# Attention outputs made transposed on column halves of TensorE, normalised before the product

## The chip, the cores and the metric

The kernel runs on one core of a Trainium2 chip. A core has five engines with an instruction queue each: TensorE (in the profile PE for its products and PEld for its weight loads), VectorE (DVE), ScalarE (ACT), GpSimd (POOL) and SyncE (SP), which here only issues transfers. Sixteen DMA engines move data. SBUF is the working memory on 128 partitions; PSUM, which takes TensorE's results, has eight banks of 2 KB per partition. Each engine executes its queue in order and waits at semaphores for the others. The metric is the device time of one execution in microseconds (us); 1 ns is a thousandth of that.

A TensorE product takes a stationary operand, loaded as weights, of up to 128 rows and 128 columns, and streams a moving operand through it: each moving column gives one result column, and the weights' columns become the partitions of the result.

## The reference

Two parts follow one another. First attention with 8 batch elements, 8 heads, 512 local and 32 global tokens, 64 numbers per head. A local token sees the 32 global tokens and the local ones at a distance of at most 32; a global token sees all 544. Then a layer of 8 experts over the 4352 resulting rows, weighted by a matrix P that eight rounds of row and column normalisation balance.

```python
s_g = scale * q_g @ k_all.T;  out_g = sm(s_g) @ v_all
s_ll = where(|i - j| <= 32, scale * q_l @ k_l.T, -1e9)
s_l = concat([scale * q_l @ k_g.T, s_ll]);  out_l = sm(s_l) @ concat([v_g, v_l])
# sm: exp(s - max) / (sum(exp(s - max)) + 1e-9)
x = concat([out_g, out_l])          # 4352 rows of 8 * 64
P = exp(x @ w_gate - max); 8 times: P /= rowsum; P /= colsum; P *= 4352 / 8
out = sum over e of P[:, e] * (relu(x @ w1[e]) @ w2[e])
```

## The kernel before

**Units.** One unit n is a batch element b and a pair of heads hp, 32 in all (four to a batch element). Its 512 queries are cut into eight blocks of 64, and one block of both heads makes 128 rows: partitions 0 to 63 are the first head's queries, 64 to 127 the second's. For that the queries stand in `qbd` block-diagonally. A block sees a window of 128 local keys and the 32 global ones, so a row of its scores has 160 numbers.

**Stages of a unit**, each a function:

- st_A transposes queries and keys into `qbd` and `kTe` (TensorE, L272, then VectorE and ScalarE copies).
- st_B makes the scores of three, three and two blocks (parts 0 to 2) on TensorE; VectorE adds the mask and takes the row's maximum in one instruction (L304, with a small read of the accumulator); ScalarE takes the exponential into `Pu` (L307). The exponentials aren't divided by their sum here. st_B0 is a form of st_B for the first four units, with the mask added by a product (L326) and one maximum per part (L331).
- st_D1 copies the 32 global columns of each row into `Pl` (POOL, L341), transposes the 128 local ones on TensorE (L344) into `ptw`, and VectorE copies the result to `pw` (L346). st_D2 transposes `Pl` (L352), and ScalarE copies it to `pg` (L354).
- st_E makes the outputs in two halves, for the even and the odd blocks (par 0 and 1): per block a product with `pw` as weights and the values as moving operand (L375) and one with `pg` and the global values (L377), accumulated into `po`. The weights' columns are the rows of both heads, and the moving operand has the values of both heads, 65 columns each: the 65th is a column of ones, so that it yields the sum of the exponentials. VectorE takes the reciprocals of the sums (L380) and multiplies the two quarters of the result that belong together into `xn` (L383).
- st_X transposes `xn` (L361), and ScalarE copies it into `xT` (L362), the transposed input of the expert layer.

Values stand in `va` (even blocks' windows), `vb` (odd blocks') and `vgz`, in which the global values stand once in each quarter of the partitions with zeros around; each has 65 columns per head.

**Global queries**, 16 groups of a batch element and four heads: st_G0 lays out queries (POOL), st_G1 makes the scores of 128 rows and 544 columns, their maximum (L408) and exponential `Pg` (L411), st_G2 transposes `Pg` (L419) into `pgs`, st_G3 makes the outputs of all four heads with five products of 260 columns (L431, L432) and scales the four matching pieces into `xgn`, by turns on ScalarE and VectorE (L441, L444); st_G4 transposes `xgn` twice in the kernel (L449) and copies it into `xT`.

**Order.** The whole order is written by hand; every engine takes its instructions in the order in which the program makes them. Units 0 to 3 are made in a first loop (L551), in which inputs land and are cast on POOL (L129, L145), and values are selected by products (L152). There the global keys of the first batch element are transposed on 32 rows of TensorE (L547), and later, at step 4, the global queries and keys of all elements on 64 rows (transpose_g: loads L192, casts on POOL L197, transposes L201). From step 4 on (loop at L601) step s does st_X of unit s - 2, st_D1, st_D2 and st_E of unit s - 1, st_B of unit s and st_A of unit s + 1. Between them stand the products of experts 0 and 1: f1 gives four products for one tile of hidden rows (p_l1, L470, relu on ScalarE or VectorE as its argument says), f2 eight products for one tile of outputs (p_l2, L484, copied by ScalarE at L487). st_G1 comes at the end of steps 4, 5, 6, 7 and every odd step from 9 to 31 (`gat`), st_G2 and st_G3 in the step after. In such a step st_D1 stands first, then two f1, st_B part 0, st_D2, st_G2. POOL also issues the value loads of the next batch element and casts its queries and keys at the end of steps.

**PSUM.** Two banks each for `mm` (p_l1, p_l2, gate logits), `sc` (scores, global outputs), and `tr` (all transposes; the tiles `pt` and `ptw`); `po` is one tile of two banks, which st_G1's scores use too. A tile waits until the readers of the earlier one in its place have ended.

After the attention follow the balancing of P, with rest work of experts 0 and 1 between its rounds, and the experts 2 to 7 (products L772 and L808 with sums and differences of operands), from about 413 us to the end.

## Time and profile before

| What | us |
|---|---|
| median of 3 runs | 1086.7 (1085.76 to 1090.41) |
| the profiled execution | 1088.94, span 1087.2 |
| TensorE busy (PE) | 1050.2, 97% of the span |
| VectorE, ScalarE, POOL busy | 697.7 (64%), 540.2 (50%), 126.6 (12%) |
| TensorE's mean granted clock | 0.991 |

All times in the profile count from the span's start. A group of instructions is named by its line, engine and operation, then what is written and read by the program's names (`po<-vb,pw`), the operands' shapes, a count, the busy time and the mean length in ns of one, and the idle time of the engine before them with what ended it. In the timeline, a line is a start, the time from the first start to the last end, and a group of up to that many like instructions in a row. TensorE pipelines its products: one of 128 moving columns is listed with 219 ns, and the next starts 56 ns later, so what a product costs the queue is the distance of starts, not its length.

### The profile page before, as it was taken

To read this page: it belongs to the slowest core of one execution; us is meant where nothing else is said; L and a number is where in the kernel's file an instruction comes from. 1 tells how busy PE (TensorE), PEld (TensorE's weight loads), DVE (VectorE), ACT (ScalarE), POOL (GpSimd) and SP (SyncE) were. 2 spreads that over 40 slices of the span, in tenths; PEclk is the share of its full clock that TensorE was granted. 3 is DMA by queue.
4 is the path that set the end of the run, shared out by engine and by line. 5 is a ranking of instruction groups with operands and counts; after the bars stand their busy time and mean duration, and the time that the engine had idled before them with its cause. 6 is when DMAs were issued, how large, how long until landed. Compare 5 with 4: busy or idle time off the path is not lost.

```text
span 1087.2 us, 19737 instructions
## 1 busy us (share of the span) xinstructions
PE 1050.2 (97%) x7988; PEld 685.3 (63%) x7988; DVE 697.7 (64%) x1504; ACT 540.2 (50%) x1091; POOL 126.6 (12%) x232
## 2 busy tenths in 40 slices
PE   7689999999999999999999999999999999999987
PEld 4555665666665455666666666666666666666676
DVE  6667676767676666768457466576575474485474
ACT  5658777777766445334334334343343343343332
POOL 7251332231401500000000000000000000000000
PEclk8989999999999999999999999999999999999999
DMA  9956676785753977423423424524424334234242
GB/s 257 195 99 168 101 170 184 114 181 145 136 103 66 215 172 289 184 97 137 174 98 136 175 97 141 185 87 175 179 99 173 137 136 175 97 136 144 104 169 79
DMA packets 102963, 160.55 MB, mean 148 GB/s; under 512 B 40909, under 2 KB 75865, under 8 KB 91865
## 3 DMA queue, kind: packets, MB, share of 16 engines
q1 hardware_dynamic: 52376, 120.03, 32.4%
q0 software_dynamic: 46736, 20.20, 15.3%
q10 hardware_dynamic: 3760, 19.08, 4.5%
q8 instruction: 62, 1.02, 0.4%
q14 instruction: 29, 0.23, 0.1%
HBM read 149.24 MB, written 33.40 MB: 168 GB/s over the span
## 4 chain that ended last, share of the span: by engine, by line
PE 81%; DVE 9%; DMA 3%; ACT 2%; issue 2%; SPq 1%; POOL 0%; DVEq 0%; ACTq 0%; POOLq 0%
PE ph L772 32%; PE m L808 20%; PE pm L808 8%; PE ph L470 8%; PE py L484 7%; DVE xn L383 3%; DMA qgf<-in_q_g_dram 1%; DVE hT L475 1%; PE sc L297 1%; PE po L377 1%; DVE ms L304 1%; PE po L375 1%; DMA pb<-pd 1%; SPq L192 1%; ACT yst L487 1%
## 5 line engine op out<-in xcount | busy, mean ns | idle before, releaser
L774 ACT ACTIVATE h<-ph 128x512 f16<-128x512 f32 (+1 forms) x432 | 247.1, 573 | 397.7 <-PE ph L772 393.8
L772 PE MATMUL ph<-xs,w1s 128*128 128x512 f16 (+1 forms) x1728 | 405.3, 367 | 3.6 <-DMA w1s<-w1d 2.3
L772 PEld LDWEIGHTS <-w1s 128*128 128x128 f16 x1728 | 169.0, 98 | 128.3 <-issue 2.6
L814 DVE SCALAR_TENSOR_TENSOR o<-pm,o 128x512 f32<-128x512 f32 (+1 forms) x106 | 70.6, 667 | 241.3 <-PE pm L808 241.0
L808 PEld LDWEIGHTS <-h 128*128 128x128 f16 x1616 | 158.1, 98 | 48.4
L808 PE MATMUL m<-w2c,s 128*128 128x256 f16 x1212 | 158.3, 273 | 0.0
L808 PEld LDWEIGHTS <-s 128*128 128x128 f16 x1212 | 118.6, 98 | 43.8
L470 PE MATMUL ph<-xT,w1e 128*128 128x512 f16 (+1 forms) x576 | 135.2, 368 | 3.7 <-DVE lg L459 1.4
L484 PE MATMUL py<-w2e,hT 128*128 128x512 f16 x544 | 128.3, 379 | 0.1
L708 DVE TENSOR_TENSOR xs<-xT,pb 128x2048 f16<-128x2048 f16 (+2 forms) x57 | 117.2, 2060 | 11.1 <-DMA pb<-pd 11.1
L808 PE MATMUL m<-w2c,h 128*128 128x256 f16 x808 | 105.5, 273 | 0.0
L808 PE MATMUL pm<-w2c,h 128*128 128x256 f16 x808 | 96.9, 273 | 0.0
L708 DVE TENSOR_TENSOR s<-h 128x2048 f16<-128x2048 f16 (+1 forms) x106 | 92.3, 912 | 4.5 <-ACT h L774 4.5
L470 PEld LDWEIGHTS <-w1e 128*128 128x128 f16 x576 | 54.6, 99 | 51.5 <-issue 6.8
L484 PEld LDWEIGHTS <-hT 128*128 128x128 f16 x544 | 50.8, 97 | 51.0 <-issue 0.2
L307 ACT ACTIVATE Pu<-ms,mx 128x160 f16<-128x160 f32 x224 | 80.8, 422 | 3.2 <-DVE mx L304 1.7
L304 DVE CUSTOM_DVE_ANT_0 ms<-sc,mask 128x160 f32<-128x160 f32 x224 | 59.7, 321 | 34.6 <-PE sc L299 17.9
L708 DVE TENSOR_TENSOR h<-h 128x1024 f16<-128x1024 f16 (+1 forms) x106 | 65.6, 660 | 0.0
L383 DVE TENSOR_TENSOR xn<-po,rr 64x256 f16<-64x256 f32 x128 | 54.0, 422 | 3.1
L473 ACT ACTIVATE hT<-ph 128x512 f16<-128x512 f32 (+1 forms) x91 | 48.9, 564 | 13.8 <-PE ph L470 11.4
L814 DVE SCALAR_TENSOR_TENSOR o<-m,o 128x512 f32<-128x512 f32 (+1 forms) x90 | 52.2, 653 | 0.4
L487 ACT COPY yst<-py 128x512 f32<-128x512 f32 x68 | 39.5, 581 | 21.0 <-PE py L484 18.7
(156 smaller groups left out, 971.1 us busy)
## 6 DMA issues: line engine op xcount, KB each, us to landing
w1s<-w1d SPq DMA_DIRECT2D x54, 1024.0 KB
yd<-yst ACTq DMA_DIRECT2D x16, 1024.0 KB
pb<-pd SPq DMA_DIRECT2D x48, 256.0 KB
o<-yd SPq DMA_DIRECT2D x8, 1024.0 KB
y<-yd SPq DMA_DIRECT2D x8, 1024.0 KB
out_dram<-o SPq DMA_DIRECT2D x8, 1024.0 KB
f<-in_q_l_dram SPq DMA_DIRECT2D x15, 512.0 KB
f<-in_k_l_dram SPq DMA_DIRECT2D x15, 512.0 KB
```

Of the source, the lines that this page charges most:

```text
L304: nc.vector.tensor_tensor_reduce(out=ms[:, ii, :], in0=sc[:, SW * ii : SW * (ii + 1)], in1=mask[:, mi, :], scale=-scale, scalar=BIG, op0=A ...
L307: nc.scalar.activation(out=d["Pu"][:, i, :], in_=ms[:, ii, :], func=AF.Exp, scale=-1.0, bias=d["mx"][:, i : i + 1])
L383: nc.vector.tensor_tensor(out=d["xn"][HB * par : HB * (par + 1), :, Dh * a : Dh * (a + 1)], in0=po[r, :, VW * a : VW * a + Dh], in1=rr[r]. ...
L470: nc.tensor.matmul(ph[:, 0:n], wts[e][0][:, dk, P * fm : P * (fm + 1)], xT[:, dk, c0 : c0 + n], start=(dk == 0), stop=(dk == DP - 1))
L473: nc.scalar.activation(out=hT[:, fm, 0:n], in_=ph[:, 0:n], func=AF.Relu)
L484: nc.tensor.matmul(py, hT[:, fk, P * c : P * (c + 1)], wts[e][1][:, fk, :], start=(fk == 0), stop=(fk == FT - 1))
L487: nc.scalar.copy(out=ys[:, c, :], in_=py)
L708: nc.vector.tensor_tensor(out=out, in0=in0, in1=in1, op=op)
L772: nc.tensor.matmul(ph[:, 0:n], w1s[i][:, dk, P * fm : P * (fm + 1)], xss[i][:, dk, 0:n], start=(dk == 0), stop=(dk == DP - 1))
L774: nc.scalar.activation(out=hs[i][:, fm, 0:n], in_=ph[:, 0:n], func=AF.Relu)
L808: nc.tensor.matmul(pm[:, HD * t : HD * (t + 1)], lhs[0][:, k, lhs[1] + P * t : lhs[1] + P * (t + 1)], w[:, q - 1, k, :], start=(k == 0 and ...
L814: nc.vector.scalar_tensor_tensor(out=o, in0=pm[:, 0 : HD * nt].rearrange("p (t d) -> p t d", d=HD), scalar=sg / float(E), in1=o, op0=ALU.m ...
```

## The change

The probabilities are divided by their sums before they meet the values, and the outputs come out of TensorE transposed.

- The exponentials on ScalarE (st_B, st_B0, st_G1) also give the sum of the row (`accum_out`), into `sm` and into a column of `m2`.
- A new stage st_N takes the reciprocals (VectorE, three, three and two at a time) and multiplies the 128 local columns of each block in place (VectorE, one instruction per block); after the last part POOL makes `Pl`, which it copied in st_D1 before, as the product of the 32 global columns and the reciprocals. st_GN does the same for a group's `Pg`: reciprocal and one multiplication on VectorE.
- st_E has the values as weights and the probabilities as moving operand: per block and head one product with 64 columns of weights and 64 moving columns, and another with the global values. The first head's results go to partitions 0 to 63, the second's to 64 to 127, so each uses one half of TensorE's columns. Both halves of blocks go into one `po` of one bank, and ScalarE copies it straight into `xT`. Reciprocals, scalings, st_X and its step are gone.
- st_G3 makes per pair of heads five products with the two heads' values as 128 columns of weights and 64 moving columns; ScalarE and VectorE copy one part each into `xT`. st_G4 and `xgn` are gone.
- The columns of ones and their memsets are gone: `va`, `vb` and `vgz` have 64 columns per head.

```diff
-                nc.scalar.activation(out=d["Pu"][:, i, :], in_=ms[:, ii, :], func=AF.Exp, scale=-1.0,
-                                     bias=d["mx"][:, i : i + 1])
+                nc.scalar.activation(out=d["Pu"][:, i, :], in_=ms[:, ii, :], func=AF.Exp, scale=-1.0,
+                                     bias=d["mx"][:, i : i + 1], accum_out=d["sm"][:, i : i + 1])
+        def st_N(n, part):
+            d = st[n]
+            i0 = 3 * part
+            i1 = min(i0 + 3, NHB)
+            if part == 0:
+                d["rs"] = att_wk.tile([P, NHB], FP32, tag="rs", name="rs")
+            nc.vector.reciprocal(out=d["rs"][:, i0:i1], in_=d["sm"][:, i0:i1])
+            for i in range(i0, i1):
+                nc.vector.tensor_scalar(out=d["Pu"][:, i, 0:KW], in0=d["Pu"][:, i, 0:KW], scalar1=d["rs"][:, i : i + 1],
+                                        scalar2=None, op0=ALU.mult)
+            if part == 2:
+                d["Pl"] = att_wk.tile([P, NHB, Sg], FP16, tag="Pl", name="Pl")
+                nc.gpsimd.tensor_tensor(out=d["Pl"], in0=d["Pu"][:, :, KW:SW],
+                                        in1=d["rs"].unsqueeze(2).to_broadcast([P, NHB, Sg]), op=ALU.mult)
         def st_D1(n):
-            d["Pl"] = att_wk.tile([P, NHB, Sg], FP16, tag="Pl", name="Pl")
-            nc.gpsimd.tensor_copy(out=d["Pl"], in_=d["Pu"][:, :, KW:SW])
...
-        def st_X(n):
-            pt = ps_tr.tile([P, NJ, P], FP16, tag="tr")
-            for j in range(NJ):
-                nc.tensor.transpose(pt[:, j, :], xn[:, j, :], identity)
-            nc.scalar.copy(out=xT[:, hp, Sl * b : Sl * (b + 1)], in_=pt.rearrange("p j q -> p (j q)"))
         def st_E(n, par):
             if par == 0:
-                d["xn"] = att_wk.tile([P, NJ, P], FP16, tag="xn", name="xn")
-            po = ps_po.tile([P, NJ, 256], FP32, tag="po")
+                d["po"] = ps_po.tile([P, Sl], FP32, tag="po", name="po")
+            po = d["po"]
             for j in range(NJ):
                 i = 2 * j + par
-                nc.tensor.matmul(po[:, j, 0 : 2 * VW], d["pw"][:, i, :], vx[:, j, 2 * hp : 2 * hp + 2, :],
-                                 start=True, stop=False)
-                nc.tensor.matmul(po[:, j, 0 : 2 * VW], d["pg"][:, i // 4, :], vz[:, i % 4, 2 * hp : 2 * hp + 2, :],
-                                 start=False, stop=True)
-            rr = att_wk.tile([P, NJ], FP32, tag="rr")
-            nc.vector.reciprocal(out=rr, in_=po[:, :, Dh])
...

+                c = slice(HB * i, HB * (i + 1))
+                for a in range(2):
+                    r = slice(HB * a, HB * (a + 1))
+                    nc.tensor.matmul(po[r, c], vx[:, j, 2 * hp + a, :], d["pw"][:, i, r], start=True, stop=False)
+                for a in range(2):
+                    r = slice(HB * a, HB * (a + 1))
+                    nc.tensor.matmul(po[r, c], vz[:, i % 4, 2 * hp + a, :], d["pg"][:, i // 4, r],
+                                     start=False, stop=True)
+            if par == 1:
+                nc.scalar.copy(out=xT[:, hp, Sl * b : Sl * (b + 1)], in_=po)
...
+        def st_GN(b, g):
+            Pg, m2 = gs[(b, g)]
+            nc.vector.reciprocal(out=m2[:, 3:4], in_=m2[:, 2:3])
+            nc.vector.tensor_scalar(out=Pg, in0=Pg, scalar1=m2[:, 3:4], scalar2=None, op0=ALU.mult)
         def st_G3(b, g):
-                nc.tensor.matmul(po[:, 0 : 4 * VW], pgs[:, t, :], vb[:, t, hs, :], start=(t == 0), stop=False)
-            nc.tensor.matmul(po[:, 0 : 4 * VW], pgs[:, 4, :], vz[:, 3, hs, :], start=False, stop=True)
+            for pr in range(2):
+                hs = slice(4 * g + 2 * pr, 4 * g + 2 * pr + 2)
+                qs = slice(HB * pr, HB * (pr + 1))
+                for t in range(NJ):
+                    nc.tensor.matmul(po[:, pr, :], vb[:, t, hs, :], pgs[:, t, qs], start=(t == 0), stop=False)
+                nc.tensor.matmul(po[:, pr, :], vz[:, 3, hs, :], pgs[:, 4, qs], start=False, stop=True)
+            t0 = GT0 * P + Sg * b
+            for a, cp in ((0, nc.scalar.copy), (1, nc.vector.tensor_copy)):
+                r = slice(HB * a, HB * (a + 1))
+                cp(out=xT[r, 2 * g : 2 * g + 2, t0 : t0 + Sg], in_=po[r, :, Sg * a : Sg * (a + 1)])
...
         for s in range(HP, NU + 1):
-                if s > HP + 1:
-                    st_X(s - 2)
-                if s > NU:
-                    break
+                if g23:
+                    st_GN(*gp)
                 st_D1(s - 1)
...
                 st_B(s, 1)
+                st_N(s, 0)
...
                 st_B(s, 2)
+                st_N(s, 1)
...
             f2("a")
-            if s == 17:
-                st_G4(0)
-            if s == NU:
-                st_G4(1)
+            if s < NU:
+                st_N(s, 2)
```

In the loop of the first four units the three parts of st_N stand together, behind st_A of the next unit.

## The prediction

> **What bounds the kernel now.** I first read the page's busy times and slices, then the busy time of the stage that the change lives in, then TensorE's timeline of one step, and last VectorE and ScalarE around the places where work moves. By stages (columns: stretch, its length, PE, PEld, DVE, ACT and POOL busy with instructions, TensorE clock, DMA share, GB/s):
>
> ```profile
> 100.00:150.00 50.00, 49.02 (x459) 30.68 (x460) 34.54 (x136) 36.40 (x86) 16.14 (x31) 1.00 0.66 145
> 200.00:250.00 50.00, 49.44 (x463) 31.00 (x461) 35.44 (x140) 37.09 (x87) 13.43 (x25) 1.00 0.66 134
> ```
>
> From about 58 to 358 us the attention steps 5 to 32 run with the expert products between them, and TensorE is busy 98% at full clock. ScalarE has 73%, VectorE 70%. So what is added to TensorE's queue there, or makes it wait, is added to the end, nanosecond by nanosecond. Before 58 us TensorE waits for landings and casts: there the chain runs over the q_g landing (12.86 us of it) and the casts behind it. The timeline gives the price of each kind of product as the distance from one start to the next (columns: start, us from first start to last end, line):
>
> ```profile
> 247.48 0.22 PE L375 MATMUL po<-vb,pw 128*128 128x130 f16 x1
> 247.54 0.22 PE L377 MATMUL po<-vgz,pg 128*128 128x130 f16 x1
> 247.60 0.61 PE L431 MATMUL po<-vb,pgs 128*128 128x260 f16 x4
> 248.04 0.27 PE L432 MATMUL po<-vgz,pgs 128*128 128x260 f16 x1
> 248.15 1.89 PE L484 MATMUL py<-w2e,hT 128*128 128x512 f16 x8
> ...
> 250.74 0.39 PE L361 MATMUL pt<-identity,xn 128*128 128x128 f16 x4
> 250.96 0.22 PE L344 MATMUL ptw<-identity,Pu 128*128 128x128 f16 x1
> ```
>
> One product of 130 columns takes 56.5 ns of the queue, one of 260 takes 110.5 (0.55 us for five), a transpose of xn 56 (0.22 us for four). Three more places of the same timeline have narrow products and products on a part of the array:
>
> ```profile
> 8.30 0.39 PE L272 MATMUL pq<-identity,qs 128*128 128x128 f16 x4
> 8.62 0.26 PE L547 MATMUL ptg<-identity,kg0h 32*128 32x32 f16 x4
> 8.81 0.23 PE L326 MATMUL sc<-m,bigI 128*128 128x128 f16 x1
> ...
> 31.72 0.39 PE L201 MATMUL pt<-identity,gs 64*128 64x64 f16 x8 [0.35 <-ACT xT L362]
> ```
>
> Eight products of 64 columns span 0.39 us and one lasts 0.19 there: (0.39 - 0.19) / 7 = 28.5 ns each. The four L272 start 56 ns apart, so the last at 8.47; L547, on 32 rows of the array, starts 0.15 later instead of 0.056, and L326 starts 0.10 after the last L547 (8.62 + 0.26 - 0.17 = 8.71) instead of the 0.026 that separates the L547s. Changing how the array is divided cost 96 and 78 ns.
>
> **The change, part by part.** The sum is against the profiled execution (1088.94 us, its span 1087.2); the median of the runs, 1086.7, lies 2.2 lower, and the sum is added to the median.
>
> 1. Transposes of the outputs go. 28 of the 32 stand in the full stage: 28 x 0.223 = 6.25 us, and 8 of st_G4, 0.45. **-6.7**.
>
> 2. Global outputs (16 times): five products of 260 columns become ten of 64 with full weights: 0.55 against 10 x 0.0285, so 16 x -0.268 = **-4.3**.
>
> 3. Local outputs: per step 16 products of 130 columns (904 ns) become 32 of 64 columns, each with a weight load of its own, half the array wide. No row has a product on half of the columns. Below: the two heads stream at once, 14.25 ns each, 28 x (456 - 904) = -12.5. Above: each narrow pair keeps the cost of a wide one, 56.5 ns, +25.3. I take 28.5 ns, the row with as many moving columns: 912 ns, 28 x 8 ns = **+0.2**. A rule of the Trainium skill speaks against that (TensorEngine Tiling (Array Packing), Restrictions and Gotchas): dividing the columns shuts off fast weight loading, and the page TensorE: Matmul & The Clock Gate, LDWEIGHTS, gives columns/1.2 ns without it, an estimated 53 ns for 64; by that this term is +22.4 and the time 1123.9. No row here loads 64 columns, so the trace can't yet say.
>
> 4. Entering and leaving the halves: st_E runs in two parts with whole-array work on both sides, four changes a step. By the L547 row 87 ns each: 28 x 4 x 0.087 = **+9.7**. Below: nothing. Above: a full emptying, a product's length less its spacing (219 - 56 = 163 ns): 18.3.
>
> 5. The normalisation of the global probabilities, st_GN, comes on VectorE ahead of st_D1's copy of ptw, and waits there for ScalarE's exponential and its sum. What is queued behind it:
>
> ```profile
> 240.52 0.71 DVE L408 TENSOR_REDUCE m<-sg 128x1 f32<-128x544 f32 x1
> 241.26 0.15 DVE L409 TENSOR_SCALAR m<-m 128x1 f32<-128x1 f32 x1
> 241.34 0.68 DVE L346 COPY pw<-ptw 128x1024 f16<-128x1024 f16 x1
> ...
> 241.51 0.71 ACT L411 ACTIVATE Pg<-sg,m 128x544 f16<-128x544 f32 x1 [2.56 <-DVE m L409]
> ...
> 242.97 0.44 PE L419 MATMUL pt<-identity,Pg 128*128 128x128 f16 x5
> ```
>
> Now L346 runs while ScalarE makes Pg, and frees ptw's bank at 242.02. There are two banks for transposes; after the change D1, D2 and G2 ask for three in a row, so G2 takes D1's and can't start before that copy has ended. The chain becomes: Pg ends 242.23, reading its sum 0.08, handing over 0.09, reciprocal 0.17, scaling 128x544 0.42 with small gaps, the copy 0.68 from 242.95, handing over: G2 at 243.7. TensorE, without the 0.22 of the transposes, is there at 242.75: it stands 0.95 us, 16 times, **+15.2**. Reading the sum is 0.08 by VectorE's accumulator row, between 0 and the 0.305 of a small ScalarE instruction (L444); the scaling lies between L409's 0.153 and the 0.69 of a 512 wide one from PSUM (L475), and I take 0.42, the share of L708's 1024 wide 0.66 in SBUF. Ends: 9.6 and 23.2.
>
> 6. Sums from the exponential, eight a step on ScalarE:
>
> ```profile
> L307 ACT ACTIVATE Pu<-ms,mx 128x160 f16<-128x160 f32 x173 | 62.3, 420 | 1.2
> L383 DVE TENSOR_TENSOR xn<-po,rr 64x256 f16<-64x256 f32 x88 | 37.2, 422 | 2.1
> L304 DVE DVE_READ_ACCUMULATOR2_ANT mx<- 128x1 f32 x171 | 14.2, 83 | 0.0
> L380 DVE RECIPROCAL rr<-po 128x4 f32<-128x4 f32 x44 | 8.0, 181 | 23.5 <-PE po L377 23.5
> L444 ACT ACTIVATE xgn<-po,rg 32x64 f16<-32x64 f32 x22 | 6.7, 305 | 8.8 <-DVE rg L434 5.0 <-DVE xgn L441 3.8
> ```
>
> The exponentials start 0.32 us apart. Three with sums delay ScalarE's copy of pg, which ends at 255.62 in a step without G2, while st_E wants it at 255.82: slack 0.2. With 0.1 each the wait is 0.1 to 0.2: 12 such steps x 0.15 = **+1.8**; with 0 each nothing, with 0.305 each 9. All in all ScalarE goes from 7.8 us of a step of 10.7 to 8.5, at most 10.2: not the bound.
>
> 7. VectorE loses 2 x (0.18 + 2 x 0.42) = 2.05 us a step and gets three reciprocals and eight scalings of 128x128 fp16: 3 x 0.18 + 8 x 0.2 = 2.1 (0.2 between L409's 0.153 and the 0.285 of L441, 32x64 from PSUM; at 0.285 the sum is 2.8). Zero: VectorE idles 3.2 us a step. Queued behind st_N are the kTe copy, which gets earlier since the po scalings ahead of it go, and the relu of f1. The next step's transposes of Pu come 4.0 us after the last score product, and part 2 needs 3.1 till then: the relu ahead 0.7, two maxima 0.6, two exponentials 0.9, reciprocal and two scalings 0.6, hand-overs 0.3. If that cover goes, each missing 0.1 us costs 2.8 in all.
>
> 8. Pl moves from st_D1 to st_N on POOL, ahead of casts and v loads issued there: it waits for the reciprocals, and those behind it are needed a step later. Zero while the wait stays under a step. SP's queue gets no new wait. The vgz transfers write whole rows instead of eight pieces, the ones columns' memsets go (0.35 us at the start), and Pl of step 1 gets up to 2.5 us later ahead of a cast that the front's chain shows. All this ends ahead of the landing of q_g, for which POOL waits 9.7 us: **0**, between -0.4 and +2.5. po is held through both halves of st_E until ScalarE's copy; the next user, st_G1, comes 3.4 us after.
>
> 9. At the end TensorE waits 0.24 for st_G4's input and 0.62 for the last xT copy; both go: **-0.9**.
>
> Sum: -6.7 - 4.3 + 0.2 + 9.7 + 15.2 + 1.8 - 0.9 = +15.0. Forecast 1101.7 us.
>
> **Rivals.**
> - Halves side by side (not slower). The two products of a pair sit on different columns and write different partitions; if they stream at once, term 3 is -12.5 and the time 1089.0. It decides below 17.8 ns a product: 28 x 32 x (0.0285 - 0.0178) = 9.6 us less leaves +5.4. The Trainium skill says so (TensorEngine Tiling (Array Packing), Key Properties): tiles run independently. The trace has no pair to test it.
> - Halves as arrays of their own (faster): they stream at once, and a half is set up without emptying the rest. Terms 3 and 4 are -12.5 and 0: 1079.3. It needs changes under 20 ns; the L547 row speaks against.
> - Free changes, 28.5 ns: 1092.0.
> - Slow narrow loads: a load of 128 columns lasts 98 ns (PEld rows); half of it, not hidden, is 49 a product: 28 x (32 x 49 - 904) = +18.6, so 1120.1. For it: 32 loads a step instead of 16. Against: L299, 32 columns wide, comes 26 ns after its neighbour with a full load hidden.
> - ScalarE binds: sums at 0.305 each: term 6 is 9, term 5 gains 3.5: 1112.4.
> - No wait at G2 (a bank free by another order): 1086.5.
>
> **How the numbers follow.** Chances: forecast 0.33, side by side 0.18, arrays of their own 0.17, free changes 0.08, slow loads 0.15, ScalarE 0.06, no wait at G2 0.03. Half a per cent, 5.4 us, is what a measurement here can tell from no change. Faster takes nearly all of the arrays of their own and some spread, 0.18; same takes side by side, half of the free changes and the last, 0.24; slower 0.58. The range goes from just under the fastest case to just over the slow loads, 1078 to 1121; the forecast alone, with term 5's and 6's ends, has 1094 to 1117.
>
> **What would show it.** The span of the eight st_E products: 16 pairs at 28.5 ns each is right, 14 or 49 a rival. The gap ahead of st_E and behind it, 0.09 each. TensorE idle ahead of the Pg transposes, 0.95 in 16 places, released by the copy of pw. The small read behind each exponential. I am wrong if the Pg transposes don't wait, or if the two heads' products overlap.

## The result, and the profile after

The changed kernel takes 1101.37 us (median, 1100.36 to 1102.6) beside 1086.23 (1084.69 to 1090.41) of the kernel before: 1.0134 times the time, with a 95% interval of 1.0103 to 1.0164. Its profiled execution took 1100.83 us with a span of 1099.1, so 11.9 of span more than the one shown of before; the kernel before spreads more from execution to execution, and the medians are 15.1 apart.

The busy table by stretches, in the changed kernel (columns as in the prediction):

```profile
100.00:150.00 50.00, 45.13 (x503) 26.31 (x496) 33.92 (x144) 36.80 (x118) 13.24 (x23) 0.97 0.68 150
200.00:250.00 50.00, 47.22 (x526) 27.48 (x520) 36.27 (x152) 37.70 (x118) 15.51 (x26) 1.00 0.61 138
```

TensorE issues more products than before (526 against 463 in the second stretch) and is busy less, 90 and 94% where it was 98 and 99. The change has taken work from the engine that bounds the stage and given it waiting time instead. VectorE and ScalarE are hardly busier, so neither has become the bound by its sum.

TensorE's timeline of one step, first half of st_E:

```profile
255.60 0.22 PE L377 MATMUL po<-pw,va 128*64 128x64 f16 x2
255.66 0.20 PE L380 MATMUL po<-pg,vgz 128*64 128x64 f16 x2
255.69 0.20 PE L377 MATMUL po<-pw,va 128*64 128x64 f16 x2
255.72 0.20 PE L380 MATMUL po<-pg,vgz 128*64 128x64 f16 x2
...
255.85 0.20 PE L380 MATMUL po<-pg,vgz 128*64 128x64 f16 x2
255.98 0.40 PE L265 MATMUL pt<-identity,ks 128*128 128x128 f16 x4
```

Each line is the pair of the two heads (x2), and a pair lasts as long as one product, so the two run at the same time; the records have their starts 2 to 4 ns apart. A new pair starts 32 ns after the one before (31.5 in the mean of the stage; only the first distance of a half is longer, 53 ns), where the prediction had 57 for a pair. From the last pair to the whole-array transposes it is 0.13 us, 0.1 more than from pair to pair: leaving the halves costs that.

The wait that the prediction put ahead of the transposes of Pg, in three engines' timelines of a step with st_G2:

```profile
251.21 0.71 ACT L410 ACTIVATE Pg<-sg,m 128x544 f16<-128x544 f32 x1 [2.75 <-DVE m L408]
251.82 0.19 ACT L410 ACTIVATION_READ_ACCUMULATOR Pg<-sg,m 128x1 f32 x1
...
252.05 0.17 DVE L416 RECIPROCAL m<-m 128x1 f32<-128x1 f32 x1 [0.93 <-ACT Pg L410]
252.25 0.36 DVE L417 TENSOR_SCALAR Pg<-Pg,m 128x544 f16<-128x544 f16 x1
252.53 0.68 DVE L354 COPY pw<-ptw 128x1024 f16<-128x1024 f16 x1
...
253.26 0.44 PE L424 MATMUL pt<-identity,Pg 128*128 128x128 f16 x5 [0.66 <-DVE pw L354]
```

VectorE stands 0.93 us behind the exponential, the copy that frees the bank starts at 252.53 instead of beside the exponential, and the transposes come 0.05 us after its end. Over the attention part the waits of TensorE on other engines are (columns: engine, what waits, what ended the wait, us in total, times, longest):

```profile
PE pt L424 <- DVE pw L354: 10.6, 15, 1.1
PE ptw L352 <- DVE Pu L341: 6.6, 17, 1.8
PE ph L462 <- DVE lg L451: 2.9, 6, 0.5
```

The first is the forecast wait. The second, transposes of Pu that wait for VectorE's scaling, was not in the sum. Its place, in the timelines of TensorE, VectorE and POOL:

```profile
260.81 0.55 PE L352 MATMUL ptw<-identity,Pu 128*128 128x128 f16 x7
261.62 0.22 PE L352 MATMUL ptw<-identity,Pu 128*128 128x128 f16 x1 [0.26 <-DVE Pu L341]
...
260.23 0.23 DVE L443 CAST xT<-pog 64x64 f16<-64x64 f32 x1 [0.85 <-ACT xT L443]
260.47 0.17 DVE L339 RECIPROCAL rs<-sm 128x2 f32<-128x2 f32 x1
260.68 0.80 DVE L341 TENSOR_SCALAR Pu<-Pu,rs 128x128 f16<-128x128 f16 x2
...
260.81 0.61 POOL L345 TENSOR_TENSOR Pl<-Pu,rs 128x256 f16<-128x256 f16 x1 [9.85 <-ACT yst L479]
```

Two scalings last 0.80 us here, and the three before them 0.58. The last one of the unit runs while POOL makes the new Pl, and ends with it; it takes 0.63 us against 0.25 of the others, in 31 of 32 units.

The long scaling alone does not make TensorE wait. From step 10 on, only the transposes that come after a step with st_G3 wait, 0.42 us each; in the steps between, the last scaling is just as long and nothing waits for it, though the transposes can come nearly as early (1.4 us after the last sum is read in step 24, 1.3 in step 23). The first of VectorE's lines above shows the difference: in a step with st_G3, VectorE's copy of the global outputs stands ahead of part 2's reciprocal, and it waits 0.85 us until ScalarE, busy with the long `xT` copy of `po`, has copied its own piece. The reciprocal starts 0.98 us after the last sum is read (260.47 against 259.49), in the other steps 0.03 us after it. Over the attention part this wait stands 15 times:

```profile
DVE xT L443 <- ACT xT L443: 13.3, 15, 1.4
```

So two things come together in the wait of the Pu transposes: a scaling longer by 0.38 us and a chain that starts about 0.95 us late. Taking away the first was tried (pl_copy, below); moving VectorE's copy was not.

To add this up I take the stage from the first transposes of unit 4's Pu to the first product of the balancing, 304.8 us before and 312.8 after, and give each distance from one TensorE start to the next to work up to the usual spacing of that kind of product, and beyond that to waiting.

| us of TensorE's queue in the stage | before | after | difference | forecast |
|---|---|---|---|---|
| transposes of the outputs (term 1) | 6.7 | 0 | -6.7 | -6.7 |
| global outputs (2) | 8.9 | 4.8 | -4.1 | -4.3 |
| local outputs (3) | 25.4 | 14.6 | -10.8 | +0.2 |
| entering and leaving the halves (4) | 0 | 11.1 | +11.1 | +9.7 |
| Pg transposes wait (5) | 1.3 | 13.0 | +11.7 | +15.2 |
| pg products wait (6) | 3.0 | 3.2 | +0.2 | +1.8 |
| Pu transposes wait (7, 8) | 0.3 | 9.9 | +9.6 | 0 |
| f1 behind the Pu transposes waits | 3.4 | 0.05 | -3.4 | none |
| waits for xn behind step 8 | 1.8 | 0 | -1.8 | none |
| f1 waits behind logits, or runs at half clock | 3.4 | 5.2 | +1.7 | none |
| end of the stage (9) | 1.2 | 0.5 | -0.6 | -0.9 |
| all others | 249.4 | 250.5 | +1.1 | 0 |
| sum | 304.8 | 312.8 | +8.0 | +15.0 |

The stretch before the stage is 2.4 us longer and the rest behind it 1.5: 11.9 in all.

Not all of the table is the change. In every profile here the granted clock reads 0.5 for one to five stretches of 3.41 us that touch the stage, and products that start in them stand up to twice as far apart. I add up what their distances have beyond the usual spacing, at most one spacing each: an estimate of 1.1 us of the stage before and 2.5 after. It lies in the rows of f1 (0.75 and 1.5) and of all others.

### The profile page after: what moved, and what is told of

Its sections match the earlier page's. It is cut to its first block, busy times and chain, and to the rows that moved or that the text cites. A ratio compares the mean times of both kernels' runs of the same rounds, so it can differ in the third digit from the quotient of the medians.

```text
span 1099.1 us, 21039 instructions
## 1 busy us (share of the span) xinstructions
PE 1047.4 (95%) x8444; PEld 668.6 (61%) x8444; DVE 711.2 (65%) x1660; ACT 555.8 (51%) x1345; POOL 132.7 (12%) x224
## 4 chain that ended last, share of the span: by engine, by line
PE 73%; ACT 11%; DVE 9%; DMA 1%; issue 1%; ACTq 0%; POOL 0%; DVEq 0%
PE ph L760 32%; PE m L796 20%; PE pm L796 8%; PE ph L462 6%; ACT Pu L301 5%; PE py L476 5%; ACT qbd L275 2%; DVE Pu L341 2%; ACT Pg L410 1%; DVE hT L467 1%; DVE m L407 1%; DVE pw L354 1%; DMA pb<-pd 1%; ACT xT L383 1%; ACT pgs L426 1%
## 5 line engine op out<-in xcount | busy, mean ns | idle before, releaser
L301 ACT ACTIVATE Pu<-ms,mx 128x160 f16<-128x160 f32 x224 | 93.6, 420 | 10.3 <-DVE mx L298 8.9
L341 DVE TENSOR_SCALAR Pu<-Pu,rs 128x128 f16<-128x128 f16 x256 | 65.9, 311 | 3.4
L479 ACT COPY yst<-py 128x512 f32<-128x512 f32 x68 | 39.4, 580 | 21.6 <-PE py L476 19.9
```

The lines of the kernel that those rows point to most:

```text
L301: nc.scalar.activation(out=d["Pu"][:, i, :], in_=ms[:, ii, :], func=AF.Exp, scale=-1.0, bias=d["mx"][:, i : i + 1], accum_out=d["sm"][:, i ...
L341: nc.vector.tensor_scalar(out=d["Pu"][:, i, 0:KW], in0=d["Pu"][:, i, 0:KW], scalar1=d["rs"][:, i : i + 1], scalar2=None, op0=ALU.mult)
L479: nc.scalar.copy(out=ys[:, c, :], in_=py)
```

## The experiments

The stage lengths and times of all kernels. The ratio is to the kernel before, measured alongside (its median was 1086.2 beside the changed kernel and 1088.2 to 1089.5 beside the others, so ratios compare better than times). The third column is the estimate just described, for each kernel's profile: it differs between profiles by up to 5 us, and differences of the stage smaller than that are read with it.

| kernel | stage, us | of it at half clock | median, us | ratio (95% interval) |
|---|---|---|---|---|
| before | 304.8 | 1.1 | 1086.23 | 1 |
| after | 312.8 | 2.5 | 1101.37 | 1.0134 (1.0103 to 1.0164) |
| after_again | 312.7 | 2.3 | 1100.55 | 1.0126 (1.0105 to 1.0147) |
| gn_late | 303.6 | 2.4 | 1092.14 | 1.0027 (1.0015 to 1.0040) |
| pl_copy | 303.8 | 0.9 | 1089.98 | 1.0004 (0.9991 to 1.0017) |
| heads_apart | 318.0 | 3.8 | 1105.45 | 1.0142 (1.0120 to 1.0164) |
| sums_alone | 308.7 | 1.6 | 1092.35 | 1.0032 (1.0015 to 1.0049) |
| both_orders | 296.2 | 1.5 | 1084.62 | 0.9965 (0.9947 to 0.9983) |
| halves_joined | 309.9 | 2.9 | 1098.48 | 1.0101 (1.0077 to 1.0125) |
| all_three | 297.1 | 5.1 | 1081.10 | 0.9943 (0.9923 to 0.9962) |
| pool_beside | 309.2 | 6.2 | 1096.93 | 1.0065 (1.0041 to 1.0090) |
| apart_both | 303.7 | 2.4 | 1090.24 | 1.0017 (1.0000 to 1.0034) |
| double_both | 309.4 | 2.4 | 1097.56 | 1.0084 (1.0056 to 1.0113) |
| best_order | 294.8 | 2.5 | 1081.42 | 0.9932 (0.9909 to 0.9954) |

### The changed kernel once more

No edit: the measure for the kernels that follow.

> The changed kernel once more, beside the others of this set: 1.011 to 1.017 of the kernel before. In its trace the stage from the first transposes of Pu of unit 4 to the first product of the balancing should again take 312 to 314 us, against 304.8 before.

Stage 312.7, the same as the first time to 0.1 us, while the stretch ahead of it differs by 1.0 (59.5 against 60.5). The stage is the sharper measure, as long as the time at half clock is kept in view, and the waits of the Pg and Pu transposes are those of the table above, 10.6 and 6.6 us by the view of the waits.

### The normalisation of Pg behind the copy of ptw

```diff
+                st_D1(s - 1)
                 if g23:
                     st_GN(*gp)
-                st_D1(s - 1)
```

> The changed kernel with one order turned: st_GN comes behind st_D1 on VectorE, so the copy of ptw no longer waits for ScalarE's exponential of the group. Theory (the bank): the Pg transposes wait because VectorE's copy of ptw, and with it the transposes' bank, is late; in the changed kernel's trace they stand 13.0 us in all, 0.8 each. Turned, the copy ends about 0.9 us earlier and what is left is the scaling of Pg itself: 0.2 us each, 3 in all. Time 10 us less than the changed kernel's 1101.4: 1091 to 1093. Rival (the chain of Pg): the transposes wait for the scaled Pg and not for a bank; then the wait stays over 0.6 each and the time within 3 us of 1101.

VectorE's and TensorE's timelines of such a step:

```profile
246.99 0.68 DVE L354 COPY pw<-ptw 128x1024 f16<-128x1024 f16 x1
248.00 0.16 DVE L416 RECIPROCAL m<-m 128x1 f32<-128x1 f32 x1 [0.33 <-ACT Pg L410]
248.20 0.36 DVE L417 TENSOR_SCALAR Pg<-Pg,m 128x544 f16<-128x544 f16 x1
...
248.62 0.45 PE L424 MATMUL pt<-identity,Pg 128*128 128x128 f16 x5
```

The copy now runs in the time in which VectorE stood, and the transposes follow the scaling of Pg. Their wait falls from 13.0 to 4.2 us, the stage by 9.2, the time by 8.4 to 9.2 in the medians, and by 10.8 to 11.6 going by the ratios. The bank of ptw, held by a copy queued behind the wait for the exponential, was the cause, as term 5 has it; what is left, 0.28 us a time, is the chain of exponential, sum, reciprocal and scaling itself.

### Pl copied by POOL instead of multiplied

VectorE scales all 160 columns, so POOL's copy has to wait for the scalings and can't run beside them.

```diff
-                nc.vector.tensor_scalar(out=d["Pu"][:, i, 0:KW], in0=d["Pu"][:, i, 0:KW], scalar1=d["rs"][:, i : i + 1],
+                nc.vector.tensor_scalar(out=d["Pu"][:, i, :], in0=d["Pu"][:, i, :], scalar1=d["rs"][:, i : i + 1],
...
-                nc.gpsimd.tensor_tensor(out=d["Pl"], in0=d["Pu"][:, :, KW:SW],
-                                        in1=d["rs"].unsqueeze(2).to_broadcast([P, NHB, Sg]), op=ALU.mult)
+                nc.gpsimd.tensor_copy(out=d["Pl"], in_=d["Pu"][:, :, KW:SW])
```

> The changed kernel with VectorE scaling all 160 columns of a block and POOL only copying the 32 global ones, so that POOL begins after the last scaling and not beside it. Theory (collision): the last scaling of a unit takes 0.63 us in place of 0.25 because POOL's product for Pl runs at that time; TensorE's transposes of Pu then wait, 9.9 us in the stage. With the copy behind, the last scaling takes 0.25 to 0.3 and the wait falls to 3 or less outside step 8: 5 to 7 us less than 1101.4, so 1094 to 1097. Rival (late sums): the scaling of part 2 starts late because of ScalarE's sums and copies; then the wait stays at 7 or more and the time within 2 us of 1101.

The scalings as groups, over the steady part of the stage; of the changed kernel:

```profile
L341 DVE TENSOR_SCALAR Pu<-Pu,rs 128x128 f16<-128x128 f16 x170 | 44.4, 314 | 2.3
```

and of this kernel:

```profile
L341 DVE TENSOR_SCALAR Pu<-Pu,rs 128x160 f16<-128x160 f16 x176 | 40.9, 285 | 3.9
```

Instructions a quarter wider are shorter in the mean, and the timelines show why:

```profile
263.29 0.43 DVE L341 TENSOR_SCALAR Pu<-Pu,rs 128x160 f16<-128x160 f16 x2
...
263.88 0.40 POOL L345 COPY Pl<-Pu 128x256 f16<-128x256 f16 x1 [2.90 <-PE ph L461]
...
264.23 0.61 PE L351 MATMUL ptw<-identity,Pu 128*128 128x128 f16 x8
```

POOL starts when VectorE has done; the last scaling takes 0.26 us in all 32 units, and the eight transposes follow one another without a gap. Their wait falls from 9.9 to 3.7 us (3.1 of that for the scalings of step 8), and the stage by 9.0, more than the 5 to 7 expected: 6.2 are that wait, 1.2 the wait of f1 behind the logits (3.7 to 2.5), 0.6 the Pg wait, which gets shorter too; the last 1.0 is f1 that does not run at half clock here. The median, 1089.98, lies under the 1094 to 1097 expected. VectorE's copy still waits for ScalarE's in the steps with st_G3 (0.83 us), and with the short scaling the chain is nevertheless just in time. That without POOL's multiplication beside the scaling the transposes come in time is shown; that it was the running side by side, and not the new form of the scaling, is tested by pool_beside.

### The two heads one after the other

```diff
-            for j in range(NJ):
-                i = 2 * j + par
-                c = slice(HB * i, HB * (i + 1))
-                for a in range(2):
-                    r = slice(HB * a, HB * (a + 1))
+            for a in range(2):
+                r = slice(HB * a, HB * (a + 1))
+                for j in range(NJ):
+                    i = 2 * j + par
+                    c = slice(HB * i, HB * (i + 1))
                     nc.tensor.matmul(po[r, c], vx[:, j, 2 * hp + a, :], d["pw"][:, i, r], start=True, stop=False)
...
```

> The changed kernel with the products of st_E in another order: all eight of the first head, then all eight of the second, so that neighbours use the same half of TensorE's columns. Theory (side by side): the two heads stream at once, a pair every 29 ns; apart, each product costs 28.5 ns alone: 32 x 28.5 against 16 x 30, +0.43 us a step, 28 steps, +12: 1113. Rival A (slow narrow loads): a load of half the columns takes 49 ns when its neighbour is on the same half: 32 x 49, +1.1 a step, +30: 1131. Rival B: the pairs' start times in the records do not show what they cost; then no change, 1101.

TensorE's timeline, first half of st_E:

```profile
260.58 0.20 PE L378 MATMUL po<-pg,vgz 128*64 128x64 f16 x1
260.62 0.20 PE L377 MATMUL po<-pw,va 128*64 128x64 f16 x1
260.65 0.20 PE L378 MATMUL po<-pg,vgz 128*64 128x64 f16 x1
260.68 0.22 PE L377 MATMUL po<-pw,va 128*64 128x64 f16 x2
260.71 0.22 PE L378 MATMUL po<-pg,vgz 128*64 128x64 f16 x2
```

A product that follows another on the same half comes 32 ns after it. But the second head's first four still run beside the first head's last four (the lines with x2, 5 to 27 ns apart), though the program has them behind: 16 products take twelve places instead of eight. So their work in the stage grows from 14.6 to 22.4 us, +7.8 and not the +12 of the expectation, and 2.7 of that are taken back by shorter waits (net of 1.3 more at half clock): the stage is 5.2 longer. In the timed ratio (1.0142 against 1.0126 and 1.0134) the intervals overlap and tell nothing apart. The direction holds, and the 32 ns rule out the rival of slow narrow loads, 49 ns a product. Here the Trainium skill differs from the trace: by "TensorEngine Tiling (Array Packing)", Restrictions and Gotchas, and "TensorE: Matmul & The Clock Gate", LDWEIGHTS, 64 columns without fast loading would take an estimated 53 ns. A load of 64 columns is listed with 112 ns here, longer than the 98 of a full one, but the loads of one half start 32 ns apart too, so their length does not set the pace.

### The sums alone

The kernel before with the sums taken by the exponentials, and read by nothing.

```diff
                 nc.scalar.activation(out=d["Pu"][:, i, :], in_=ms[:, ii, :], func=AF.Exp, scale=-1.0,
-                                     bias=d["mx"][:, i : i + 1])
+                                     bias=d["mx"][:, i : i + 1], accum_out=d["sm"][:, i : i + 1])
...
```

> The kernel before, with the exponentials also giving their sums, which nothing reads. Theory (hidden): an exponential and its read are 0.41 us from start to start in place of 0.32, 0.09 x 8 = 0.74 us more of ScalarE's time a step, which idles 2.9 us a step; the wait for pg in front of st_E is at most 0.1 in 12 steps: within 2 us of the kernel before. Rival (ScalarE binds): its copies come late and TensorE waits for pg or for a product's bank: 5 us or more.

A miss: 0.32% slower, stage +3.9. Of the kernel before, in the waits of all engines:

```profile
PEld L377 <- ACT pg L354: 3.0, 2, 1.6
```

and of this one:

```profile
PEld L379 <- ACT pg L356: 10.2, 27, 1.9
```

The waits of these two views count an idle weight load; in the queue of TensorE the products with pg wait 6.2 us in 30 places instead of 3.0 in 2. So term 6 is a true mechanism: the copy of pg stands behind exponentials that have become longer, 0.41 us from start to start instead of 0.32. It costs 3.1 us, where the prediction had 1.8, but in the kernel before; in the changed kernel it costs 0.2, because ScalarE has no xT copy left at the beginning of the step. That last reason is read from the order of the program and was not tried by itself.

### Both orders mended

gn_late and pl_copy together.

> The two edits together: st_GN behind st_D1, and Pl copied by POOL behind the last scaling. Alone they took 9.2 and 9.0 us from the stage of 312.8. Theory (two waits of their own, at the Pg transposes and at the transposes of Pu): they add, 293 to 296 us in the stage, and the time is 0.986 to 0.991 of the kernel before. Rival (one slack behind another): TensorE, released at one place, waits at the next, so that together they give less than 13 us: a ratio of 0.995 to 1.0.

Stage 296.2, at the edge of what was expected: 16.6 less than the changed kernel, where the two alone give 18.2. So the two waits stand side by side and share little. With them gone the change is a gain: ratio 0.9965, 15.9 us less than the changed kernel, and 8.6 less stage than before. The ratio was expected lower, 0.986 to 0.991, and lies where the rival had it; but the rival's reason, together less than 13 us, doesn't hold. 2.3 us of the stage's gain are lost ahead of it (60.3 against 58.1); the rest of the gap to the ratio stays open.

### The two halves of st_E joined

st_E(s - 1, 0) directly ahead of st_E(s - 1, 1), in the changed kernel: two changes between the whole array and its halves a step less.

```diff
             f2("a")
-            if s > HP:
-                st_E(s - 1, 0)
...
             if s > HP:
+                st_E(s - 1, 0)
                 st_E(s - 1, 1)
```

> The changed kernel with both parts of st_E behind st_B's last part, next to one another, so that TensorE changes between whole array and halves twice a step and not four times. Theory (each change costs about 0.09 us): 28 x 2 x 0.09 = 5 us less, plus up to 3 more because the transposes of Pu get 0.3 us more cover: 1101.4 less 5 to 8. Rival (the gaps around the halves are gaps of the records, or drains that other work fills): within 2 us of the changed kernel.

Less than expected: the stage is 2.9 us shorter, the time 2.1 less, where 5 to 8 were forecast and the rival had at most 2. The two gaps a step are gone, 5.0 us between them (2.6 ahead of the next unit's transposes of keys, 2.4 behind f2). But scores and VectorE's chain come no earlier and TensorE reaches the transposes of Pu sooner: their wait grows from 9.9 to 11.7, and waits of f1 by 1.4. In the steps with st_G3, VectorE's copy of the global outputs now waits longer for ScalarE, 19.6 us in all instead of 13.3. So the price of term 4 is confirmed, and in this kernel 2.1 of the 5.0 are lost again, mostly to other waits.

### All three

both_orders with the halves joined.

> All three edits: st_GN behind st_D1, Pl copied, halves joined. Theory: the gains add, 24 us less than the changed kernel in all: 0.981 to 0.987 of the kernel before. Rival (with the parts joined, ScalarE's copy of po comes later, just ahead of st_G1, which wants po's bank): the third edit gives nothing more, 0.987 to 0.991.

A miss: 0.9943, above the rival's range too, and no gain over both_orders in the stage as it stands (297.1 against 296.2). The steady step is 0.08 us shorter, where two changes would give 0.18; the transposes of Pu wait 6.1 us in 35 places, up from 3.6 in 13. The first step of the stage, step 5, takes 12.1 us instead of 9.7: the granted clock is 0.50 there from 57.3 to 64.2 us, and eight products of f1 span 3.62 us. Without the time at half clock the stage would be 292.0 against 294.7, an estimate, so the third edit gives about 2.7. The intervals of the two ratios overlap.

### POOL busy beside VectorE's scaling

both_orders, with a multiplication on POOL into a spare tile where the changed kernel had the one that made Pl (`bigI2` is a tile of ones); the copy of Pl stands behind it.

```diff
+                spare = att_wk.tile([P, NHB, Sg], FP16, tag="spare", name="spare")
+                nc.gpsimd.tensor_tensor(out=spare, in0=bigI2, in1=d["rs"].unsqueeze(2).to_broadcast([P, NHB, Sg]), op=ALU.mult)
                 nc.gpsimd.tensor_copy(out=d["Pl"], in_=d["Pu"][:, :, KW:SW])
```

> The kernel with both orders mended (stage from the first transposes of Pu of unit 4 to the first product of the balancing: 296.2 us), plus a product on POOL whose result nothing reads, issued like the changed kernel's: as soon as part 2's reciprocals are there, beside VectorE's last two scalings. Pl is still copied behind it. Theory (collision): the last scaling of a unit takes 0.63 us again and TensorE's wait inside the transposes of Pu, 3.6 us with both orders mended, is 9 or more: stage 301 to 304. Rival (it was the late Pl, or the wider scaling, that helped): the last scaling stays at 0.26 and the stage at 296 to 298.

Timelines of VectorE and POOL:

```profile
268.26 0.60 DVE L343 TENSOR_SCALAR Pu<-Pu,rs 128x160 f16<-128x160 f16 x3
...
269.45 0.79 DVE L343 TENSOR_SCALAR Pu<-Pu,rs 128x160 f16<-128x160 f16 x2
...
269.56 0.62 POOL L348 TENSOR_TENSOR spare<-bigI,rs 128x256 f16<-128x256 f16 x1 [2.42 <-DVE rs L341]
```

The multiplication shares no tile with the scalings except the reciprocals, which both read, and the last scaling is long again: 0.62 us in 21 of 32 units. The Pu transposes wait 9.2 us instead of 3.6, and the stage is 13.0 longer, more than the 5 to 8 that were expected. So it is POOL's running beside VectorE that lengthens the scaling, not a dependence. The Trainium skill has this, and the trace agrees: "SBUF — State Buffer", section "SBUF: two separate sides", says that the two engines share a pair of ports, which one of them holds for a whole instruction. In the changed kernel the last scaling indeed ends 0.05 us after POOL's multiplication. The stage loses 13.0 and not 5.6 because other things come on top: 4.7 us are more time at half clock (6.2 against 1.5), and the Pg transposes and f1 behind the logits wait 1.1 each more. Without the time at half clock the loss is 8.4.

### The heads apart, without the two waits

heads_apart's edit in both_orders, so that no wait takes the difference back.

> Both orders mended, and st_E's products by heads, eight of the first and then eight of the second. On the changed kernel this put 7.8 us more into TensorE's issue time (25 ns a product in place of 16), but the measured times of the two could not be told apart. Theory (the issue time counts where TensorE binds): here, with fewer waits in which to hide, the stage is 6 to 9 us longer than 296.2. Rival (it is hidden, or the records mislead): within 3 us of 296.2.

Stage +7.5, ratio 1.0017 against 0.9965. What took back 2.7 us in heads_apart were the waits; with few of them left the products cost nearly what their spacing says (22.4 against 14.6 us of work).

### Every product of st_E twice

```diff
+            for twice in range(2):
                 for j in range(NJ):
...
```

> Both orders mended, and every product of st_E made twice over, the second time into the same place: the cost of the products by itself, without further changes between halves and whole array. Theory (a pair every 29 to 30 ns): 32 more products are 16 pairs, 0.48 us a step, 28 steps: 13 to 14 us more in the stage, 309 to 311. Rival (a product costs what one of 64 whole-array columns costs, 28.5 ns): 25 us more, 321.

Stage +13.2, as expected, and far from the rival's 25. 16 pairs more in each of 28 steps are 448; in the records they start 31.6 ns apart in the mean, 14.2 us of work, so 15.8 ns a product. The stage grows by 1.0 less, since other waits get shorter (13.2 / 448 = 29.5 ns a pair is what is left net). This is the price of term 3 without further changes between halves and whole array.

### A better order

both_orders with the halves joined from step 9 on, st_G2 behind part 1's scores, and one more f1 in step 8.

```diff
+            if s < NU:
+                st_B(s, 1)
             if g23:
...
-            if s > HP:
+            if HP < s <= 2 * HP:
                 st_E(s - 1, 0)
...
+                if s > 2 * HP:
+                    st_E(s - 1, 0)
                 st_E(s - 1, 1)
...
-            if s > 2 * HP:
+            if s >= 2 * HP:
                 f1("v")
```

> Both orders mended; the two parts of st_E joined from step 9 on only (in the earlier steps joining cost 3 us); st_G2 behind st_B's second part, where the 0.23 us that its transposes still wait are covered; and one set of expert products more in step 8, where TensorE waits 3.3 us for the last scalings. Theory: joined -3 to -5, st_G2 -3, step 8 -3: 9 to 11 us less than 296.2 in the stage, and a ratio of 0.986 to 0.990 to the kernel before. Rival (each wait taken away shows the next one on ScalarE's or VectorE's side): less than 5 us, a ratio over 0.992.

A miss, and the rival's case: the Pg wait all but goes (0.5 us), and the transposes of Pu wait 7.5 in its place. The stage is 294.8, 1.4 less than both_orders and not 9 to 11, though it holds one f1 more (four products, 0.9 us). At 0.9932 (0.9909 to 0.9954) it is faster than the kernel before and the changed one, and not to be told from all_three.

## Why the prediction was right, and where only its sum was

The forecast was 1101.7 us and the time is 1101.4. That the two agree to 0.3 us is luck: two of the steps were wrong by about 10 us each, in opposite directions, and by its own sign the prediction is wrong there ("I am wrong if the Pg transposes don't wait, or if the two heads' products overlap": they wait, and the products overlap). The stage itself came out at +8.0 instead of +15.0. The 7.0 are made up by the front (2.4), the rest behind the stage (1.5), and medians 3.2 further apart than the profiled executions, none of which is in the sum.

- **Terms 1 and 2** hold: -6.7 and -4.1. Ten narrow products with full weights take 29 ns each, the price taken from the eight products on 64 rows.
- **Term 3 failed**: "I take 28.5 ns, the row with as many moving columns". That is near the price of a pair, 31.6 ns, but the two products of a pair run at once, as the first rival had it. (The sentence "16 pairs at 28.5 ns each is right" doesn't fit the term, which has 32 products at 28.5, so 57 a pair; and its upper end, +25.3, is 56.5 ns for each narrow product, not for each pair.) The term is -10.8 instead of +0.2. The runs with the heads apart and with the products doubled show it from both sides: 32 ns behind a neighbour on the same half, 31.6 ns a pair. The choice went to the row with the same moving columns, though no row had products on different columns. The Trainium skill's "TensorEngine Tiling (Array Packing)", Key Properties, by which tiles run independently, agrees with these runs.
- **Term 4** holds: 11.1 against 9.7, with 0.10 us a change instead of 0.087. The rival that had the halves as arrays of their own, side by side with free changes, falls at this.
- **Term 5** holds in mechanism and nearly in size: 15 waits of 0.87 instead of 16 of 0.95. Reading the sum delays the next step by 0.09 (taken 0.08), the scaling takes 0.36 (taken 0.42). gn_late shows that the order is the cause.
- **Term 6** is 0.2 instead of 1.8 here. Its mechanism is real, and costs 3.1 in the kernel before.
- **Terms 7 and 8 failed**: "Zero: VectorE idles 3.2 us a step", and Pl on POOL "Zero while the wait stays under a step". I looked at POOL's new place for who waits for it, and not for what runs beside it. The scaling taken as 0.2 us is 0.25 alone, and 0.63 beside POOL's multiplication. The sum of 3.1 us that part 2 needs also leaves out what stands ahead of its reciprocal in a step with st_G3: VectorE's new copy of the global outputs, which waits 0.85 us for ScalarE's. The cover of 4.0 us was not enough for both together; with either one alone it is, as the steps without st_G3 show on one side (long scaling, early chain) and pl_copy on the other (short scaling, late chain). Behind step 8, where less stands between, it was not there: 3.5 of the 9.9 us are in that place. "If that cover goes, each missing 0.1 us costs 2.8" counts all 28 steps; the cover went in the steps with st_G3 alone, 0.42 us each.
- **Not in the sum**: a gain of 3.4 where f1 waited behind the Pu transposes, one of 1.8 behind step 8 where transposes waited for xn, and a loss of 1.7 in f1, 1.0 in waits behind the logits and 0.7 at half clock.
- **The front** was put at 0 between -0.4 and +2.5 and is 2.4 longer (1.4 in the second profile). Its length moves between 57.1 and 63.7 us among the kernels run here, the time at half clock in it between 10 and 27 us, and which of its parts did it stays open. So does why the medians differ by 15.1 and the profiled executions by 11.9; the time of the kernel before spreads over more than 5 us.

So the forecast's case, slower because of new waits and changes of the array, came true, but with the rival's price for the products. Had term 3 alone been right, the sum would have been 1090.7; with the Pu wait too, 1100.3.

## What to carry to other kernels

When an operation moves to another engine, look not only for who waits for it but for what runs beside it: here a POOL instruction of 0.6 us that nobody was waiting for lengthened VectorE's, and without it the stage was 9 us shorter. Look also for what the other engine's queue does to a copy that two engines share: by the trace, VectorE's late copy was the other half of that wait. An instruction that waits for another engine belongs behind the copy that frees a bank, not ahead of it; swapping two lines gave 9 us. And the work that is saved on the engine that bounds a stage is a gain only when its inputs come earlier too: with 21.6 us of TensorE's products gone and up to 11.1 paid for the changes of the array, the kernel was 1.3% slower or 0.7% faster, by order and by which engine multiplies.

## What the runs showed of the hardware that was not expected

- Two products with 64 columns of weights each, on different halves of TensorE's columns, start 2 to 4 ns apart, and a new pair every 31.6 ns. Products that stand behind in the program run beside earlier ones when they use the other half (heads_apart).
- Going from the whole array to halves or back costs about 0.10 us each time, 11.1 us for 28 steps of four changes.
- A multiplication of 128x128 fp16 numbers by one number per row in SBUF takes 0.25 us on VectorE alone, and 0.63 beside a POOL instruction of 0.61, ending 0.05 us after it.
- Reading the sum of an exponential is listed as an instruction of 0.19 us on ScalarE, and delays the next instruction by 0.09.
- Behind step 8 of the changed kernel, after waits of 0.65 and 1.84 us, eight products of f1 span 2.87 us, where 1.9 is usual, while the granted clock is 0.50 from 107.1 to 110.5 us. In pl_copy TensorE stands 3.1 us at the same place, and the clock stays at 1.00 from 104 to 110 us; so such a wait does not always bring it down, and what does stays open.
